# Transposes of q and x moved from TensorE to VectorE in an attention and SwiGLU kernel

## Chip, core and metric

The kernel runs on one core of a Trainium2 chip. The metric is the device time of one execution in microseconds (us), as the median of several runs. Before the change it is 1030.94 us (three runs, 1030.42 to 1032.77). TensorE's granted clock was 1.000 over the whole profile.

Names of the profile: PE is TensorE (matmuls), PEld its weight loads, DVE is VectorE, ACT is ScalarE, POOL is GpSimd, SP is the engine whose queue issues most transfers. "L712" is line 712 of the kernel before; after the change most lines are two higher.

## What is computed

Linear attention without softmax, with a root-mean-square norm for each head, and then a feed-forward block:

```python
kv  = einsum('bhsd,bhse->bhde', k, v)          # batch 8, 8 heads, 576 positions, 64 wide
out = einsum('bhsd,bhde->bhse', q, kv)
x   = out / sqrt(mean(out*out, -1) + 1e-6) * g_norm
x   = x.transpose(0, 2, 1, 3).reshape(4608, 512)
g   = x @ w_gate                               # 512 x 1536
h   = g / (1 + exp(-g)) * (x @ w_val)
y   = h @ w_out                                # 1536 x 512
```

## The kernel before

The 4608 rows are cut into nine blocks of 512 (`blocks`, n = 0 to 8). A block's rows can straddle two batches, so its q comes from two pieces. For each block there is an attention part (class `Att`) and a feed-forward part (class `Ffn`) with an up stage (gate and value products) and a down stage (product with w_out). The attention part of block n+1 is done inside the down stage of block n, between its matmuls.

**Fewer products.** The big matrix products use a Strassen-like scheme: seven products P1 to P7 of half-sized blocks in place of eight, at the price of sums of the operands. S1, S3, S4 and the changed a21 are sums of the moving operand (`sums` for x, `h_sums`, `turn_s3` and the last line of `after2` for h; the last of these is called S4). T2 is a sum of the weights that is made once, in place, in the value weights `wv` (`t2`): one subtraction and one addition for each of six pairs j. Block 0 makes its up stage plainly (`plain_up`), while weights still come in. Block 1 uses the scheme once (class `Up`), and blocks from `DEEP` = 2 on use it twice, one within the other (class `Inner`). The doubled scheme needs further weight sums, called leaves. They are made by VectorE during block 1 (`leaf_steps`) from the weights, stored to DRAM (`w<-t`, `w<-r`, `w<-xi`, L821) and read back by every later block in pieces through the class `Stream` (`t<-w`, L793). GpSimd makes the remaining weight differences (`prepare`, `turn_t`, L112) in the pool `t_pool` with nine tiles, which stream pieces share: `stream.pump` issues a load when the tile that stood nine places earlier is free. `stream.enable(n + 1)` opens a block's loads.

**Order.** Each engine runs its instructions in the order of its queue. A scheduler orders them at build time from the order of the source and from its own view of readiness; `tc.issue_after(x)` holds back what is in its scope until x in that order. TensorE's order in a down stage comes from the loop in `Ffn.down`: with the step list of an attention part that has an entry for 5, it is P1, P6, P5, P7, P2, P4, P3, otherwise P1, P5, P6, P7, P2, P4, P3. After each P the entry of `nxt.steps()` for it is run.

**Two ways for q and x.** The matmuls want q and x with the head dimension on partitions; they come in and go out with rows on partitions.
- On TensorE: q is loaded by rows (`load_q`, four transfers a block), transposed by matmuls with an identity matrix (`turn_q`, L335) and copied out of PSUM. x is transposed in the same way (`turn_x`, L402) and copied out by ScalarE with the gain (L403). Each takes 16 transposes a block. The steps are `half` at P1, `middle` at P6 and `last` at P2: the two halves of the block are normed one after the other.
- On VectorE: q is loaded by 32 small transfers that already put each 32-wide quarter where it belongs (`load_quarters`, L281), so that one instruction a half (STREAM_TRANSPOSE, L329) turns all 32 x 32 blocks in place. For x, two such instructions turn the blocks (`blocks_x`, L412), 16 transfers move them to their partitions (`place_x`, L426, eight each on the queues of SP and ScalarE), and ScalarE applies the gain (`gain_x`, L431). The steps are `whole` at P1 (both products, the norm of all 512 rows, the block transposes), `place_x` at P5 and `end` (gain and sums) at P2.

`TURNED` = 3 is the first block of the second way; block 1 takes the second way for its q alone. In the first way q of a block is loaded late in the up stage before it; in the second it is loaded a block earlier still: `blocks[n + 2].load_q` runs at the start of the down stage of block n.

**Block 0 and 1.** T2 of all six pairs follows the first scaled half of block 1 (`nxt.halves[0]`). In block 1 the leaves of the last two pairs (`latest`) are made behind P1 and P7 of the down stage, both in one buffer named `xi`.

Of the kernel before, what the change touches and what calls it, by code (L numbers as in the profile page):

```python
# [8 lines left out]
F32 = mybir.dt.float32  # L9
# [5 lines left out]
P = 128  # L15
# [3 lines left out]
def kernel(  # L19
# [41 lines left out]
    nc = tc.nc  # L61
# [22 lines left out]
    ld_pool = pool("ld", 4)  # L84
# [23 lines left out]
    wg, wv = ([consts.tile([P, NS, 2 * P], F32, name=f"{x}{j}") for j in range(NP)] for x in ("wg", "wv"))  # L108
# [84 lines left out]
    class Att:  # L193


        def __init__(self, n):
            self.n = n

            self.cut, half = divmod(n, 2)
            self.split = half * D  # L200
            self.ps, self.z = {}, None
            self.q, self.k, self.v, self.room = [], {}, {}, None
            self.halves = []
            self.quarters = n == 1 or n >= TURNED

        def parts(self, t):

# [58 lines left out]
                    )  # L266
                    views[j] = t.rearrange("p h (t d) -> p h t d", t=KT)

        def load_quarters(self, i):


            ld = ld_pool.tile([P, LD], F32, name="ld")[:, 0 : 2 * BLK]
            to = ld.rearrange("p (j g d) -> p j g d", j=2, d=P // 4)
            cut = 2 * self.n
            spans = [(self.n - 1, S - D * self.n, 0, cut), (self.n, 0, cut, BLK // 32)]
            for j in range(2):
                for r in range(4):
                    h, d = divmod(r, 2)
                    for b, s0, g0, g1 in spans:
                        if g1 > g0:  # L280
                            nc.sync.dma_start(  # L281
                                out=to[32 * r : 32 * (r + 1), j, g0:g1],
                                in_=q[b, 4 * i + 2 * j + h, s0 : s0 + 32 * (g1 - g0), 32 * d : 32 * (d + 1)].rearrange(
                                    "(g p) d -> p g d", p=32
                                ),
                            )
            self.q.append(ld)

        def load_q(self, i):
            if self.quarters:  # L290
# [127 lines left out]
        def place_x(self):  # L418
            src = self.turned.rearrange("p i (x c) -> p (i x) c", c=P)
            self.x = x_pool.tile([P, 7, 2, HB], F32, name="x")  # L420
            dst = self.x[:, 0:4].rearrange("p o k (t c) -> p (o k t) c", c=P)
            rows = [slice(32 * r, 32 * (r + 1)) for r in range(4)]
            for a in range(4):
                for b in range(4):
                    queue = nc.scalar if b % 2 else nc.sync
                    queue.dma_start(out=dst[rows[b], :, rows[a]], in_=src[rows[a], :, rows[b]])  # L426

        def gain_x(self):
            for i in range(2):
# [56 lines left out]
        def steps(self):  # L486
# [14 lines left out]

            if self.n >= TURNED:
                return {1: whole, 5: self.place_x, 2: end}
# [19 lines left out]

    DEEP = 2

    TURNED = 3

    class Quad:

# [41 lines left out]
    class Up(Quad):  # L571
# [51 lines left out]
        def multiply(self, p):  # L623
            super().multiply(p)
            ffn = self.ffn
            if ffn.n != DEEP - 1:
                return

            if p == 5:
                self.leaf_room = ring().rearrange("p f (s c) -> p (f s) c", c=P)  # L630
            if p in (5, 7, 4):
                at = 3 * (5, 7, 4).index(p)
                ffn.making.extend(leaf_steps(self.j, [(self.w[p].unsqueeze(1), (p,))], self.leaf_room[:, at:]))
            if p == 3:
                if ffn.leaf_room is None:
                    ffn.leaf_room = x_pool.tile([P, 3, 7, P], F32, name="xi").rearrange("p a b c -> p (a b) c")
                halves = lambda t: t[self.j].rearrange("p (o i) c -> p o i c", o=2)
                steps = leaf_steps(self.j, [(halves(wg), (1, 2)), (halves(wv), (6, 3))], ffn.leaf_room)
                if self.j < NP - 2:
                    ffn.later.extend(steps)  # L640
                else:
                    ffn.latest.append(steps)

# [195 lines left out]
    class Down(Quad):  # L839
# [23 lines left out]
        def multiply(self, p):  # L863
            super().multiply(p)
            if p in self.t:
                stream.free((self.ffn.n, p))
            if p == 4:
                stream.enable(self.ffn.n + 1)
            stream.pump()

# [20 lines left out]
        def after2(self):  # L891
            add(nc.vector, self.o1[:, :, 0:HD], self.ps["a"], self.s)
            if self.final:
                self.ffn.store(self.o1[:, :, 0:HD], 0, slice(0, HD))

            pairs = self.ffn.h.rearrange("p (j e) t -> p e j t", e=2)
            sub(nc.vector, pairs[:, 1, :, 0:HB], pairs[:, 1, :, 0:HB], pairs[:, 0, :, HB:BLK])

        def after7(self):
            o = ring()  # L900
# [25 lines left out]
    class Ffn:  # L926
# [52 lines left out]
        def down(self, nxt):  # L979

            down = self.down_
            fill = nxt.steps() if nxt else {}
            for p in (1, 6, 5, 7, 2, 4, 3) if 5 in fill else (1, 5, 6, 7, 2, 4, 3):
                if p == 1:
                    down.turn_t(7, self.ended)
                if p == 6:
                    down.turn_t(4, nxt.halves[0] if nxt and nxt.n >= TURNED else None)

                with tc.issue_after(nxt.multiplied.ins) if self.n == 0 and p in (5, 6) else ExitStack():
                    down.multiply(p)  # L990
                self.make(12)
                if p == 5 and self.n == DEEP - 1:
                    for i in range(2):
                        self.loads(i)
                if p in fill:
                    fill[p]()
                if p in (1, 7) and self.latest:

                    with tc.issue_after(nxt.scaled.ins):
                        for step in self.latest.pop(0):  # L1000
                            step()
                if p == 1:

                    with tc.issue_after(nxt.q_turned.ins) if self.n == 0 else ExitStack():
                        down.turn_s3()
# [47 lines left out]
    def t2(place, b22, b11):  # L1053

        sub(nc.vector, place, b22, place)
        add(nc.vector, place, place, b11)

    blocks = [Att(n) for n in range(NB)]
# [7 lines left out]
    for n in range(NB):  # L1066
        ffn = Ffn(n, blocks[n])
        nxt = blocks[n + 1] if n + 1 < NB else None
        if n == 0:

            with tc.issue_after(squared.ins), tc.issue_after(scaled.ins):
                weights(2)
            ffn.plain_up(0, (0,))
            copied = blocks[0].copied
            blocks[0].turn_x(1)
            for f in range(NF):
                with tc.issue_after(blocks[0].copied.ins if f else copied.ins):
# [12 lines left out]
            ffn.plain_end()  # L1090
            for g in range(2):
                nxt.kv(g)
        else:

            def third():
                nxt.kv(0)
                nxt.load_kv(1)

            def two_thirds():
                nxt.kv(1)  # L1100
                if nxt.n < TURNED:
                    for i in range(2):
                        nxt.load_q(i)

            ffn.up({4: third, 8: two_thirds} if nxt else {})
        if nxt:
            nxt.turn()
        if 0 < n < NB - 2:
            blocks[n + 2].load_kv(0)
        if TURNED - 2 <= n < NB - 2:  # L1110
            ffn.loads = blocks[n + 2].load_q
            if n >= DEEP:
                for i in range(2):
                    ffn.loads(i)
        ffn.down(nxt)
        if n == 0:
            blocks[2].load_kv(0)

            with tc.issue_after(nxt.halves[0].ins):
                for j in range(NP):  # L1120
                    t2(wv[j][:, 0:2], wv[j][:, 2:4], wg[j][:, 0:2])


# [29 lines left out]
```

## Time and profile before

| Part of the run | start to end, us | length, us |
|---|---|---|
| loads, block 0's attention, weights and up | 0 to 117.79 | 117.79 |
| down of block 0, attention of block 1 inside | 117.79 to 159.85 | 42.06 |
| up of block 1, leaves made | 159.85 to 238.62 | 78.77 |
| down of block 1, attention of block 2 inside | 238.62 to 279.66 | 41.04 |
| blocks 2 to 8 | 279.66 to 1031.2 | 751.5 |

The borders are starts of TensorE's matmuls: P1 of a down stage (b<-wo,h) and the first product of an up stage. The profile's section on busy time has one entry for each engine: microseconds, share of the span, number of instructions. The chain that ended last is followed back from the last instruction, so it tells whose work the end waited for. In the list of waits each line gives the engine and line that waited, what it waited for, the total, the number of times and the longest.

In up of block 1 VectorE is busy 70.3 of 78.8 us and GpSimd 32.0, in down of block 0 37.5 and 19.5 of 42.1, in down of block 1 30.7 and 10.2 of 41.0. SP's queue issued 21 small loads of q in 11.69 us at 109.65, and eight placements of x in 5.76 us at 693.77. The median time from issue to landing was 2.0 us for most of the small q loads, 3.2 us for a placement, 3.6 us for a stream load of 256 KB.

### The profile page before, as it was taken

How to read it: one execution, taken by the hardware profiler on the slowest of the kernel's cores; microseconds unless marked ns; L12 is line 12 of the kernel's file. 1: busy time of each engine (PE TensorE's matmuls, PEld its weight loads, DVE VectorE, ACT ScalarE, POOL GpSimd, SP SyncE). 2: the span in 40 equal slices, each digit the busy share in tenths (PEclk: the TensorE clock that was granted, in tenths of full speed). 3: DMA queues.
4: the chain of work that ended last, by engine and by line, in shares of the span. 5: the costliest groups of instructions: out<-in, count | busy, mean ns of one | idle time of the engine just before them, and what ended most of it. 6: DMA issues, size and time to landing. Idle time of an engine off the chain costs nothing.

```text
span 1031.2 us, 21440 instructions
## 1 busy us (share of the span) xinstructions
PE 1013.0 (98%) x8570; PEld 903.5 (88%) x8570; DVE 703.9 (68%) x1185; ACT 230.2 (22%) x359; POOL 371.6 (36%) x280
## 2 busy tenths in 40 slices
PE   5999999999999999999999999999999999999998
PEld 4544688888899989998999899988999899989997
DVE  2999796997766855585657576674669466856661
ACT  2666111222211211221112122111212111211110
POOL 0000543444035612462156305630455136513670
PEclk9999999999999999999999999999999999999999
DMA  7689614783778456855686468736862666066611
GB/s 215 195 261 266 119 37 128 186 223 72 205 202 248 90 133 209 248 126 114 192 242 163 68 205 240 198 53 186 236 199 50 169 196 193 22 165 205 189 30 41
DMA packets 252403, 168.15 MB, mean 163 GB/s; under 512 B 129168, under 2 KB 220432, under 8 KB 252304
## 3 DMA queue, kind: packets, MB, share of 16 engines
q1 hardware_dynamic: 225808, 163.37, 57.9%
q10 hardware_dynamic: 26432, 3.41, 2.0%
q8 instruction: 68, 1.11, 0.5%
q14 instruction: 31, 0.25, 0.1%
q0 software_dynamic: 64, 0.00, 0.0%
HBM read 138.02 MB, written 22.41 MB: 156 GB/s over the span
## 4 chain that ended last, share of the span: by engine, by line
PE 83%; DVE 10%; DMA 4%; SPq 1%; ACT 1%; issue 1%; DVEq 0%; ACTq 0%
PE b L712 26%; PE b L549 20%; PE c L712 13%; PE c L549 10%; PE a L712 6%; PE a L549 5%; DVE r L153 2%; PE m L355 1%; PE m L314 1%; SPq L281 1%; DVE r L147 1%; DMA h<-in_v_dram 1%; DVE r L152 1%; DMA ld<-in_v_dram 1%; DVE xi L112 1%
## 5 line engine op out<-in xcount | busy, mean ns | idle before, releaser
L111 POOL TENSOR_TENSOR r<-r 128x256 f32<-128x256 f32 (+1 forms) x105 | 110.7, 1060 | 310.1 <-DVE r L111 204.4
L111 DVE TENSOR_TENSOR r<-b,r 128x512 f32<-128x512 f32 (+1 forms) x273 | 162.1, 606 | 64.2 <-PE b L712 59.1
L112 POOL TENSOR_TENSOR t<-wo 128x512 f32<-128x512 f32 x81 | 117.1, 1470 | 191.6 <-DVE wo L111 106.9
L111 DVE TENSOR_TENSOR r<-c,r 128x512 f32<-128x512 f32 (+1 forms) x179 | 108.5, 618 | 95.0 <-PE c L712 55.5
L712 PE MATMUL b<-x,t 128*128 128x128 f32 x1092 | 151.0, 275 | 0.0
L712 PEld LDWEIGHTS b<-x,t 128*128 128x128 f32 x1092 | 136.5, 192 | 0.6
L111 DVE TENSOR_TENSOR r<-a,r 128x512 f32<-128x512 f32 (+1 forms) x99 | 62.5, 631 | 108.7 <-PE a L549 63.0
L712 PE MATMUL c<-xi,t 128*128 128x128 f32 x840 | 112.2, 275 | 0.4 <-DVE xi L111 0.4
L113 POOL TENSOR_TENSOR h<-r 128x1024 f32<-128x1024 f32 (+1 forms) x40 | 82.1, 2067 | 80.6 <-DVE r L111 72.8
L712 PEld LDWEIGHTS c<-xi,t 128*128 128x128 f32 x840 | 102.8, 192 | 0.5 <-DVE xi L111 0.5
L549 PE MATMUL b<-wo,h 128*128 128x256 f32 x432 | 99.5, 382 | 0.1
L549 PE MATMUL b<-t,h 128*128 128x256 f32 x432 | 96.9, 381 | 0.0
L549 PEld LDWEIGHTS b<-t,h 128*128 128x128 f32 x432 | 81.3, 190 | 11.3 <-issue 0.2
L549 PEld LDWEIGHTS b<-wo,h 128*128 128x128 f32 x432 | 79.9, 190 | 12.8 <-DVE h L113 2.5
L726 ACT COPY r<-b 128x512 f32<-128x512 f32 x63 | 36.9, 585 | 211.7 <-PE b L712 199.8
L712 PE MATMUL b<-xi,t 128*128 128x128 f32 x588 | 79.7, 276 | 0.0
L712 PEld LDWEIGHTS b<-xi,t 128*128 128x128 f32 x588 | 72.4, 192 | 0.0
L712 PE MATMUL b<-x,wg 128*128 128x128 f32 x336 | 52.7, 279 | 0.2 <-DVE x L112 0.2
L712 PE MATMUL b<-x,wv 128*128 128x128 f32 x336 | 51.3, 275 | 0.0
L549 PE MATMUL c<-t,s 128*128 128x256 f32 x216 | 48.3, 380 | 0.0
L549 PE MATMUL a<-wo,h 128*128 128x256 f32 x216 | 48.3, 379 | 0.0
L549 PE MATMUL c<-wo,h 128*128 128x256 f32 x216 | 48.1, 379 | 0.0
(131 smaller groups left out, 1579.8 us busy)
## 6 DMA issues: line engine op xcount, KB each, us to landing
t<-w SPq DMA_DIRECT2D x336, 256.0 KB, 3.6
out_dram<-r SPq DMA_DIRECT2D x17, 512.0 KB, 3.1
ld<-in_k_dram SPq DMA_DIRECT2D x26, 288.0 KB, 5.1
ld<-in_v_dram SPq DMA_DIRECT2D x26, 288.0 KB, 5.7
ld<-in_moe_w_gate_dram SPq DMA_DIRECT2D x12, 512.0 KB, 4.6
ld<-in_moe_w_val_dram SPq DMA_DIRECT2D x12, 512.0 KB, 4.4
ld<-in_moe_w_out_dram SPq DMA_DIRECT2D x12, 512.0 KB, 5.3
w<-t SPq DMA_DIRECT2D x18, 256.0 KB, 2.5
```

Of the source, the lines that this page charges most:

```text
L111: add = lambda e, o, a, b: e.tensor_tensor(out=o, in0=a, in1=b, op=OP.add)
L112: sub = lambda e, o, a, b: e.tensor_tensor(out=o, in0=a, in1=b, op=OP.subtract)
L113: mul = lambda e, o, a, b: e.tensor_tensor(out=o, in0=a, in1=b, op=OP.mult)
L147: nc.vector.tensor_scalar(out=mag.bitcast(F32), in0=mag.bitcast(F32), scalar1=self.LOW, scalar2=self.HIGH, op0=OP.max, op1=OP.min,)
L152: nc.vector.tensor_scalar(out=sign, in0=high, scalar1=0x80000000, scalar2=None, op0=OP.bitwise_and)
L153: return nc.vector.scalar_tensor_tensor(out=mag, in0=mag, scalar=3, in1=sign, op0=OP.logical_shift_left, op1=OP.bitwise_xor)
L281: nc.sync.dma_start(out=to[32 * r : 32 * (r + 1), j, g0:g1], in_=q[b, 4 * i + 2 * j + h, s0 : s0 + 32 * (g1 - g0), 32 * d : 32 * (d + 1)]. ...
L314: nc.tensor.matmul(self.kv_ps[r][u * D : (u + 1) * D, g, :], lhsT=k[:, u, c, :], rhs=v[:, u, c, :], start=(c == 0), stop=(c == KT - 1),)
L355: self.multiplied = nc.tensor.matmul(self.ps[i][u][p : p + D, t, j, :], lhsT=self.qt[rows, 2 * i + t, j, p : p + D], rhs=kvs[b % 3][rows, ...
L549: nc.tensor.matmul(banks[e][:, e], lhsT=lhsT, rhs=rhs, start=first and i == 0 and (e == 0 or banks[0] is not banks[1]), stop=i == self.ste ...
L712: nc.tensor.matmul(ps[:, i, f], lhsT=self.weight(o, p, f), rhs=self.operand(o, p), start=first and (i, f) == (0, 0), stop=True, skip_group ...
L726: nc.scalar.copy(out=dst, in_=ps)
```

## The change

Blocks 1 and 2 take the second way, for q and for x: `TURNED` becomes 1 and `quarters` holds for every block but block 0. What goes with it:
- Block 3's q isn't loaded in down of block 1 but in up of block 2, in four parts (`load_quarters` gets the pairs to load).
- Block 2's q is still loaded in up of block 1, now by quarters.
- The leaves of the last two pairs of block 1 are made behind P5 and P7, after the placement of x is issued; the second takes a ring buffer in place of `xi`.
- Half of T2 (pairs 3 to 5) is put behind S4 of block 0's down stage, to leave VectorE to x before.
- A block's stream loads may begin behind P7, not behind P4.
- With `TURNED` = 1 the condition in `turn_t(4, ...)` also holds in block 0: the difference waits for the scaled x of block 1.

It is meant to take transposes off TensorE and to keep what replaces them off its way.

```diff
-            self.quarters = n == 1 or n >= TURNED
+            self.quarters = n > 0
...
-        def load_quarters(self, i):
+        def load_quarters(self, i, pairs=(0, 1)):
-            ld = ld_pool.tile([P, LD], F32, name="ld")[:, 0 : 2 * BLK]
-            to = ld.rearrange("p (j g d) -> p j g d", j=2, d=P // 4)
+            if pairs[0] == 0:
+                self.q.append(ld_pool.tile([P, LD], F32, name="ld")[:, 0 : 2 * BLK])
+            to = self.q[i].rearrange("p (j g d) -> p j g d", j=2, d=P // 4)
...
-            for j in range(2):
+            for j in pairs:
...
-    TURNED = 3
+    TURNED = 1
...
-                steps = leaf_steps(self.j, [(halves(wg), (1, 2)), (halves(wv), (6, 3))], ffn.leaf_room)
+                steps = lambda room: leaf_steps(self.j, [(halves(wg), (1, 2)), (halves(wv), (6, 3))], room)
...
-            if p == 4:
+            if p == 7:
                 stream.enable(self.ffn.n + 1)
...
-                if p == 5 and self.n == DEEP - 1:
-                    for i in range(2):
-                        self.loads(i)
                 if p in fill:
                     fill[p]()
-                if p in (1, 7) and self.latest:
-                    with tc.issue_after(nxt.scaled.ins):
-                        for step in self.latest.pop(0):
+                if p in (5, 7) and self.n == DEEP - 1:
+                    with tc.issue_after(nxt.scaled.ins), tc.issue_after(nxt.placed.ins):
+                        room = self.leaf_room if p == 5 else ring().rearrange("p f (s c) -> p (f s) c", c=P)
+                        for step in self.latest.pop(0)(room):
                             step()
...
-                if nxt.n < TURNED:
+                if nxt.n == 2:
                     for i in range(2):
                         nxt.load_q(i)
-            ffn.up({4: third, 8: two_thirds} if nxt else {})
+            fill = {4: third, 8: two_thirds} if nxt else {}
+            if n == DEEP:
+                for a, at in enumerate((1, 2, 3, 5)):
+                    fill[at] = lambda i=a // 2, j=a % 2: nxt.load_quarters(i, (j,))
+            ffn.up(fill)
...
             with tc.issue_after(nxt.halves[0].ins):
-                for j in range(NP):
+                for j in range(NP // 2):
+                    t2(wv[j][:, 0:2], wv[j][:, 2:4], wg[j][:, 0:2])
+            with tc.issue_after(ffn.down_.s4.ins):
+                for j in range(NP // 2, NP):
                     t2(wv[j][:, 0:2], wv[j][:, 2:4], wg[j][:, 0:2])
```

More of the change, by code (lines that the diff above doesn't have):

```diff
@@ L286, in load_quarters @@
                             )
-            self.q.append(ld)
         def load_q(self, i):
@@ L425, in place_x @@
                     queue = nc.scalar if b % 2 else nc.sync
-                    queue.dma_start(out=dst[rows[b], :, rows[a]], in_=src[rows[a], :, rows[b]])
+                    placed = queue.dma_start(out=dst[rows[b], :, rows[a]], in_=src[rows[a], :, rows[b]])
+                    if b % 2 == 0:
+                        self.placed = placed
         def gain_x(self):
@@ L637, in multiply @@
                 halves = lambda t: t[self.j].rearrange("p (o i) c -> p o i c", o=2)
-                steps = leaf_steps(self.j, [(halves(wg), (1, 2)), (halves(wv), (6, 3))], ffn.leaf_room)
+                steps = lambda room: leaf_steps(self.j, [(halves(wg), (1, 2)), (halves(wv), (6, 3))], room)
                 if self.j < NP - 2:
-                    ffn.later.extend(steps)
+                    ffn.later.extend(steps(ffn.leaf_room))
                 else:
@@ L896, in after2 @@
             pairs = self.ffn.h.rearrange("p (j e) t -> p e j t", e=2)
-            sub(nc.vector, pairs[:, 1, :, 0:HB], pairs[:, 1, :, 0:HB], pairs[:, 0, :, HB:BLK])
+            self.s4 = sub(nc.vector, pairs[:, 1, :, 0:HB], pairs[:, 1, :, 0:HB], pairs[:, 0, :, HB:BLK])
         def after7(self):
@@ L1109 @@
             blocks[n + 2].load_kv(0)
[L1110 to L1114, printed above, removed]
+        if DEEP <= n < NB - 2:
+            for i in range(2):
+                blocks[n + 2].load_q(i)
         ffn.down(nxt)
```

## The prediction

> **What bounds the kernel now.** I read the page's busy shares first, then the chain that ended last, then what TensorE waited for, then the timelines around the places that the change touches.
>
> ```profile
> PE 1013.0 (98%) x8570; PEld 903.5 (88%) x8570; DVE 703.9 (68%) x1185; ACT 230.2 (22%) x359; POOL 371.6 (36%) x280
> PE 83%; DVE 10%; DMA 4%; SPq 1%; ACT 1%; issue 1%; DVEq 0%; ACTq 0%
> ```
>
> TensorE is busy for 98% and owns 83% of the chain. TensorE's waits say how much is left besides its own work:
>
> ```profile
> PE m L248 <- DMA h<-in_v_dram: 5.8, 2, 4.9
> PE b L335 <- DMA ld<-in_q_dram: 4.2, 1, 4.2
> PE a L712 <- DMA t<-w: 0.8, 1, 0.8
> PE c L549 <- DVE r L111: 0.7, 1, 0.7
> ```
>
> 10.0 us lie in the start (first loads), which the diff leaves alone. All later waits are below 1 us each. So a matmul taken off TensorE shortens the run by its issue time, as long as nothing new stops it. The transposes to be removed, in TensorE's timeline (start, length, count, operation):
>
> ```profile
> 135.65 1.04 PE L402 MATMUL m<-ident,r 128*128 128x128 f32 x8
> ...
> 148.62 1.04 PE L402 MATMUL m<-ident,r 128*128 128x128 f32 x8
> ...
> 233.07 0.60 PE L335 MATMUL m<-ident,ld 128*128 128x128 f32 x4
> ...
> 237.75 0.60 PE L335 MATMUL m<-ident,ld 128*128 128x128 f32 x4
> ...
> 255.46 1.04 PE L402 MATMUL m<-ident,r 128*128 128x128 f32 x8
> ...
> 268.42 1.04 PE L402 MATMUL m<-ident,r 128*128 128x128 f32 x8
> ```
>
> Lengths overlap [...]; what counts is the distance between starts.
>
> [...] starts follow at 0.216 us (128x256) and 0.112 us (128x128) almost everywhere. [...] each L412 pair is followed by 16 transfers (L426). [...] two T2 subtractions took 1.28 us at 130.88, two took 3.44 us at 133.28, while GpSimd ran L112 (132.94 to 137.85).
>
> **The parts.**
>
> *1. x of blocks 1 and 2 and q of block 2 leave TensorE.* I compare the down stages by starts. Block 0: P1 starts at 117.79, the next up at 159.85: 42.06 us. A stage of the new kind is read from block 2 (P1 to up at 387.97): both products together 2.02 us (353.84 to 355.86), the product P after them 5.28, each other P 5.18. New block 0: P1 5.38 + the wait for the second L329 (0.46 idle, 0.67 by starts), which stays because the loads of block 1's q are the same + 2.02 + 5.28 + 5 x 5.18 = 39.25. Saved 2.81. Block 1: 238.62 to 279.66 is 41.04; new 5.28 + 2.02 + 5.28 + 25.90 = 38.48. Saved 2.56. The 16 transposes of q in up of block 1 took 0.44 + 0.49 + 0.22 + 0.44 + 0.44 = 2.03 by starts. **Sum 7.40 us**, all on the chain.
>
> *2. What replaces them beside TensorE.* VectorE: 2 q transposes of 1.23 us for one copy of 0.69 (L339), and per block two x transposes (2.36 the pair). The way of x in block 2, which I take as the pattern:
>
> ```profile
> 364.69 2.36 DVE L412 STREAM_TRANSPOSE r<-r 128x1024 f32<-128x1024 f32 x2
> ...
> 367.13 6.73 ACTq L426 DMA_DIRECT2D x<-r  x8
> ...
> 377.32 2.19 ACT L431 ACTIVATE x<-x,gain 128x1024 f32<-128x1024 f32 x2 [2.84 <-DMA x<-r]
> ...
> 379.76 0.68 DVE L111 TENSOR_TENSOR x<-x 128x512 f32<-128x512 f32 x1
> ```
>
> From the end of the products (355.86) to placed and scaled x (379.51) 23.65 us; the up stage follows 32.1 us after the products. In block 0 the products end at 123.17 + 0.67 + 2.02 = 125.86, so x is scaled at 149.5, and VectorE comes out of S4 and the add behind it at 149.7; up starts at 159.85 - 2.81 = 157.0. S1 of x is first read by P5, one P of 1.73 later (158.7).
>
> *3. Half of T2 behind S4.* Six T2 (12 instructions) took 11.5 us of VectorE, 130.88 to 142.41. Now three stand before S4, three after it (P2 ends at about 146.6, S4 at 149). Queued between these three (3 x (0.73 + 1.04) = 5.3 us bare, up to 8.7 at the contended 3.44 + 2.36 for two) are the four sums of x (2.8 us bare, 5.8 contended: 151.11 to 156.82 in the trace). In the built order S1 stands behind three of the six T2 instructions: 149.7 + 2.5 + 0.7 = 152.9 bare, 149.7 + 4.6 + 1.7 = 156.0 contended, against 158.7. Hidden both ways, with 2.7 us left at the worst; a21 (P6, 160.5) has less. I keep 0.3 us for it, less than a quarter of one GpSimd subtraction (1.34).
>
> *4. q of block 2 in quarters.* 32 loads for 4, on SP. In block 0, 21 of these took 11.69 us, 0.56 each, so 32 need 18 us. They stand among the 48 stores of leaves (L821), which wait on VectorE in order; the last 16 stand together in the built queue and hold the stores behind them by 16 x 0.52 (20 took 10.36 at 238.73) = 8.3 us, less the 1.8 us by which the next store follows anyway (213.38, 215.15): 6.5. Behind a store wait a GpSimd difference that reuses its tile (L112 waited 26.5 us for these in five waits) and a leaf buffer. SP catches up by about 222; the q transposes run near 227, the down stage reads near 237. I cost it at nothing, hidden behind up of block 1; the upper bound is 6.5 us less the 3.1 us that GpSimd already waits for such a store at 221.59: 3.4.
>
> *5. Block 3's q in up of block 2, not in down of block 1.* SP work of 32 x 0.56 in a stretch where SP waits for TensorE to free stream tiles. Nothing. It clears SP for the 8 placements there; in block 5 the same loads ended at 693.77 and put placements off to then.
>
> *6. Last leaves behind P5 and P7, the last in a ring buffer.* 16 VectorE instructions after the x transposes, 6.6 us (a set took 3.30, 253.62 to 256.92). In the pattern VectorE is idle 9.84 us there (367.05 to 376.89); the last four (2.0 us) come after S4 and push the sums of x back by as much. The first xi sum would end at 382.53 + 1.02 + 2.0 = 385.6 on the pattern's clock, where P5 reads it at 388.86. Nothing.
>
> *7. Stream loads begun behind P7.* In the order of the queues this changes one place: down of block 5, where the first loads stood behind an output store.
>
> ```profile
> 706.88 0.41 SPq L936 DMA_DIRECT2D out_dram<-r  x1
> 707.40 4.96 SPq L793 DMA_DIRECT2D t<-w  x9
> ...
> 713.82 0.71 PE L712 MATMUL a<-x,t 128*128 128x128 f32 x4 [0.79 <-DMA t<-w]
> ...
> 717.67 2.05 PE L712 MATMUL c<-xi,t 128*128 128x128 f32 x16 [0.39 <-DVE xi L111]
> ```
>
> Now six loads follow the placements directly (699.5). The wait of 0.8 us goes. The next two (0.39 and 0.20) stay: the scaling L431 still stands behind the copy L907 in ScalarE's queue and ran at 706.75. **0.8 us.**
>
> Sum: 7.4 + 0.8 - 0.3 = 7.9; 1030.94 - 7.9 = **1023.0**.
>
> **Rivals.** *A crowded SP in block 1*: the stores come late, GpSimd's differences and VectorE's adds slip, P5 of a unit waits. For it: TensorE already waits 0.74 there for VectorE (213.98), and VectorE is busy 70.3 of 78.8 us. Against: the delay falls late and is made up. 1030.94 - 8.2 + 3.4 = 1026.1. *x late*: placements spread out by traffic, or sums held by contention, in blocks 1 and 2; P5 stands second in the up stage and nothing can go ahead of it. For it: VectorE's queue is in order and the sums of block 1 now share it with T2. Against: 2.7 us left. Four us in each: 1022.7 + 8 = 1030.7, no change. *Slower*: both of these, and 6 us in each block: 1022.7 + 12 = 1034.7. It takes a placement of about 9 us more than the 23.65 measured. *Better*: the waits of block 1 (0.9 + 0.2 by starts) and the two at 717 go too: 1021.0.
>
> **How the numbers follow.** Forecast 0.58, better 0.08, crowded SP 0.22, x late 0.08, slower 0.04. The range takes in the first three: 1021.0 to 1027.0, leaving out 0.12. Faster 0.88, within 0.2% (1028.9 to 1033.0) 0.08, slower 0.04.
>
> **What would show it.** No L402 after the start and no L335 after 40 us; the down stages of blocks 0 and 1 near 39.3 and 38.5 us; no wait of TensorE for t<-w near 706; VectorE some 7 us busier. Wrong would be: waits of TensorE above 1 us at the first P5 of blocks 1 or 2, waits for VectorE in up of block 1 above the 1.1 us of now, or L329 waiting for q in block 1.

## The result, and the profile after

The changed kernel takes **1025.23 us** (median of four runs, 1025.01 to 1026.59) against 1031.03 (1030.42 to 1032.77) for the kernel before on the same chip: ratio 0.9944, 95% interval 0.9927 to 0.9961. It is 5.8 us faster where 7.9 were forecast. A repeat, told below, gave 0.9946 (0.9934 to 0.9959).

The profiled executions differ by more, 1031.2 and 1023.2. Of this difference of about 7.9 us, 1.45 lie ahead of P1 of block 0, in the wait for the first loads, which put P1 at 117.79 us before, at 116.34 after and at 117.44 in the repeat, and has nothing to do with the change. So I compare from P1 of block 0 to the last instruction: 913.14 before, **906.68** after (907.14 in the repeat), **6.0 to 6.5 us saved**.

The page's busy shares and its chain by engine, after:

```profile
PE 1006.5 (98%) x8522; PEld 896.9 (88%) x8522; DVE 701.0 (69%) x1168; ACT 228.0 (22%) x352; POOL 368.9 (36%) x280
PE 92%; DVE 3%; DMA 2%; SPq 1%; issue 1%; ACT 1%; DVEq 0%; ACTq 0%
```

TensorE has 48 matmuls fewer (16 for q, 32 for x) and owns 92% of the chain where it had 83%. Its waits after (engine, what was waited for, us, times, longest):

```profile
PE m L248 <- DMA h<-in_v_dram: 4.7, 2, 3.9
...
PE c L551 <- DVE r L111: 1.6, 3, 0.7
```

The wait for t<-w is gone. The wait for VectorE's running sum, 0.7 in one place before, is 1.6 in three: that is the first sign of where gain was lost. Stage by stage, from matmul start to matmul start ("spread" is the experiment x5, "spread twice" x11; a row named for a block has its up and its down stage):

| Stage | before | after | repeat | spread | spread twice |
|---|---|---|---|---|---|
| down of block 0 | 42.06 | 39.51 | 39.78 | 39.50 | 39.50 |
| up of block 1 and P1 of its down stage | 84.05 | 82.76 | 82.96 | 81.88 | 81.96 |
| rest of down of block 1 | 35.76 | 34.13 | 34.13 | 34.13 | 34.13 |
| block 2 | 108.31 | 108.49 | 108.49 | 107.83 | 107.83 |
| block 6 | 109.65 | 108.43 | 108.44 | 108.55 | 106.86 |
| P1 of block 0 to the end | 913.14 | 906.68 | 907.14 | 905.24 | 903.63 |

Block 6 runs from the first product of its up stage to that of block 7; it is what the texts below call the stretch from block 5 to 6. Blocks 3 to 5, 7 and 8 agree to 0.05 us in every kernel, so a single profile shows a stage's change well, while the whole time does not. Two stages are exceptions. Up of block 1 moves by 0.6 us between profiles of like kernels (84.05 and 83.44 before; 82.41 to 82.96 after). Down of block 0 carries a wait of TensorE for block 1's second q transpose (L329), whose loads land at varying times: by starts it cost 0.67 us before, nothing after, 0.29 in the repeat and 0.93 in x2.

**The account.** TensorE's time from each start to the next, summed by line from down of block 0 to the end of block 2, before and after: attention products of blocks 1 and 2 (L355) 6.19 and 4.06; transposes of x (L402) 3.68 and 0; of q (L335) 2.02 and 0. That is 7.83 us taken off. The kv products (L314) rise from 5.56 to 6.29, the P products from 250.82 to 252.62 (1.2 of these 1.8 us in up of block 1, 0.4 in block 2): 2.53 us come back. 5.30 remain, and with 1.22 at block 6 the sum is 6.5. The attention products fall because each block's stood in two groups before, one of them with the 0.67 us wait for L329 in it, and now stand in one of 2.03. That this wait is gone is luck, and 0.67 of the 6.5 us with it. The kv products stood in five groups and now stand in eight; by estimate every group costs some 0.24 us beyond its matmuls, from the times of three groups after (72 at 202.38 took 1.21, 34 at 144.66 took 0.72, 14 at 317.37 took 0.38).

**The way of x in block 1**, beside TensorE, in the timelines of VectorE, ScalarE and TensorE after (start, length, engine, operation):

```profile
131.28 2.36 DVE L412 STREAM_TRANSPOSE r<-r 128x1024 f32<-128x1024 f32 x2
...
133.72 7.41 ACTq L426 DMA_DIRECT2D x<-r  x8
...
143.38 2.19 ACT L433 ACTIVATE x<-x,gain 128x1024 f32<-128x1024 f32 x2 [1.62 <-DMA x<-r]
...
157.58 1.89 PE L551 MATMUL c<-x,t 128*128 128x256 f32 x8
```

The first P5, at 157.58, has no bracket, so it waits for nothing. x is scaled at 145.57, 21.8 us after the products end (123.75), and its last sum ends at 156.3.

**The lost part**, at the end of up of block 1 after, one line each from the timelines of SP, SP, VectorE and TensorE:

```profile
209.60 9.55 SPq L282 DMA_DIRECT2D ld<-in_q_dram  x16
219.25 0.42 SPq L823 DMA_DIRECT2D w<-r  x1
...
222.90 1.03 DVE L112 TENSOR_TENSOR xi<-wv 128x512 f32<-128x512 f32 x2 [0.92 <-DMA w<-xi]
...
232.31 1.99 PE L551 MATMUL c<-x,wv 128*128 128x256 f32 x8 [0.55 <-DVE r L111]
```

Sixteen q loads hold SP for 9.55 us. The leaf stores (L823) behind them go out late; VectorE waits 0.92 us to write a new leaf into a buffer that such a store still reads; and everything in VectorE's queue slips, the running sum included that P3 of the last unit needs. Four profiles have this run of 16 loads at over 9 us, and in them VectorE's wait for the store and TensorE's stall at the last unit (by starts) go together: 0.92 and 0.71, 0.68 and 0.48 in the repeat, 0.59 and 0.37 in x6, 0.61 and 0.39 in x9.

### The profile page after: what moved, and what is told of

The parts are those of the page before. It is cut to its first block, busy times and chain, and to the rows that moved or that the text cites. A ratio compares the mean times of both kernels' runs of the same rounds, so it can differ in the third digit from the quotient of the medians.

```text
span 1023.2 us, 21404 instructions
## 1 busy us (share of the span) xinstructions
PE 1006.5 (98%) x8522; PEld 896.9 (88%) x8522; DVE 701.0 (69%) x1168; ACT 228.0 (22%) x352; POOL 368.9 (36%) x280
## 4 chain that ended last, share of the span: by engine, by line
PE 92%; DVE 3%; DMA 2%; SPq 1%; issue 1%; ACT 1%; DVEq 0%; ACTq 0%
PE b L714 26%; PE b L551 20%; PE c L714 13%; PE c L551 10%; PE a L714 6%; PE a L551 5%; PE b L1018 4%; PE c L1018 4%; PE m L314 2%; PE m L355 1%; DMA h<-in_v_dram 1%; SPq L282 1%; DVE xi L112 1%; DVE r L111 1%; DMA h<-in_k_dram 0%
## 5 line engine op out<-in xcount | busy, mean ns | idle before, releaser
L112 POOL TENSOR_TENSOR t<-wo 128x512 f32<-128x512 f32 x81 | 114.5, 1437 | 213.4 <-DVE wo L111 103.5
```

## Experiments

All are edits of the changed kernel unless said otherwise. "From P1" is the time from P1 of block 0 to the end in the profile; 906.7 to 907.1 for the changed kernel.

**The changed kernel again (x0_after_again).** No edit.

> The changed kernel once more, for a narrower interval and to see which stage lengths repeat. Its trace gave 8.0 us less than that of before, of which 1.45 lay in the start (first loads), while the timed medians differ by 5.8. If the start is chance, the ratio is near 0.9940 to 0.9945 and the stages repeat: down of block 0 39.5 us, up of block 1 with P1 82.8, rest of down of block 1 34.1. If the start belongs to the change, P1 of block 0 again comes about 1.4 us earlier than before.

1025.56 us (1024.57 to 1027.35), ratio 0.9946 (0.9934 to 0.9959). The stalls near 195 and 209 us and at the last unit of up of block 1 were 0.76, 0.89 and 0.48 us by starts, in the first profile 0.50, 0.90 and 0.71. The loss comes each time, its parts vary. P1 of block 0 came at 117.44, near the 117.79 of before, so the earlier start in the first profile was chance.

**Block 2's q back on TensorE (x1_q2_on_tensor).**

```diff
-            self.quarters = n > 0
+            self.quarters = n > 0 and n != 2
```

> Block 2's q by rows and transposed on TensorE as before the change, its x still on VectorE. Measured by up of block 1 with P1 of its down stage (84.05 before, 82.76 changed, 81.54 if only what was taken away counted; 1.22 lost). Theory (the 1.22 is the price of q by quarters and on VectorE): the 16 transposes cost 2.03 again and the 1.22 comes back, 83.6. Rival (the loss comes from the rest of the change, such as the other order of P1 or the split of kv): 84.8.

1026.78 us (1026.40 to 1027.17), ratio 0.9957 (0.9941 to 0.9972). Up of block 1 with P1 is 83.44, with one stall near 211 (0.89); block 2 is 107.83; from P1 906.67. That is the theory's 83.6, not the rival's 84.8. So taking q of block 2 off TensorE, 2.02 us of matmuls, earned nothing as it was built: the 0.5 to 0.7 that it gained in up of block 1 was lost in block 2, which here is 0.66 shorter, with its kv products in one group fewer.

**Block 2's q by four large loads (x2_q2_few_loads).** Loads by rows, transposes still on VectorE: block 2 then computes with q in the wrong places, and only the times are of use.

```diff
         def load_quarters(self, i, pairs=(0, 1)):
...
+            if self.n == 2:
+                for t in range(2):
+                    tile_ = self.q[i][:, BLK * t : BLK * (t + 1)].rearrange("p (h d) -> p h d", h=H)
+                    for b, s0, p0, p1 in self.parts(2 * i + t):
+                        nc.sync.dma_start(out=tile_[p0:p1], in_=q[b, :, s0 : s0 + p1 - p0, :].rearrange("h p d -> p h d"))
+                return
```

> Block 2's q in 4 large loads by rows in place of 32 small ones, still transposed by VectorE, so block 2's rows of the output are those of a misplaced q (that part of the computation is changed). It takes the crowd off SP and leaves VectorE's two transposes. Theory SP (stores of leaves come late behind 16 loads in a row, VectorE waits 0.92 us for one and is late with an add): up of block 1 with P1 81.6 to 81.9, no wait of VectorE for w<-xi, in all about 1.0 us less than the changed kernel. Theory VectorE (2.45 us more work in a full stage): 82.6 to 82.8, the wait of 0.71 us before P3 of the last unit stays.

1024.72 us (1023.45 to 1026.13), ratio 0.9937 (0.9923 to 0.9950); up of block 1 with P1 82.42, block 2 107.83, from P1 906.57. The stall at the last unit is gone, as the SP theory wants, but the stage is between the two expectations: the stalls near 196 and 210 (0.84 and 0.88) stayed. Down of block 0 was 40.44, since the products waited for L329, 0.93 us by starts. Inconclusive on the size.

**Half of the loads on ScalarE's queue (x3_two_queues).**

```diff
-                            nc.sync.dma_start(
+                            (nc.scalar if self.n == 2 and d else nc.sync).dma_start(
```

> Half of block 2's 32 loads of q issued from ScalarE's queue, so that SP has 16. Theory SP: the longest run of loads on SP halves, up of block 1 with P1 about 82.0, if 16 issues of 0.5 to 0.8 us on ScalarE don't hold its copies out of PSUM. Theory VectorE: 82.7. If ScalarE's copies are held: over 83, with waits of TensorE for copies by ScalarE.

1026.05 us (1024.80 to 1027.75), ratio 0.9950 (0.9937 to 0.9964); up of block 1 with P1 82.95, from P1 907.36 (1.04 of it in down of block 0, at the wait for L329). ScalarE's timeline and TensorE's:

```profile
188.33 2.66 ACTq L282 DMA_DIRECT2D ld<-in_q_dram  x4
191.03 0.59 ACT L571 COPY r<-b 128x512 f32<-128x512 f32 x1 [4.11 <-DMA ld<-in_q_dram]
...
191.76 1.97 PE L551 MATMUL b<-x,t 128*128 128x256 f32 x8 [2.23 <-ACT r L571]
```

The stalls for VectorE are gone, all three, but a copy out of PSUM stands behind four loads in ScalarE's queue, and TensorE waits 2.23 us for it. This wait comes ahead of the three places and gives VectorE time there, so the run doesn't tell what the shorter run of loads on SP is worth. Here four loads on the queue of an engine that also computes took 2.66 us ahead of that copy.

**Only block 1's x, on the kernel before (x4_block1_x_alone).**

```diff
-            if self.z is None or 0 < self.n < TURNED:
+            if self.z is None or self.n == 2:
...
-            if self.n >= TURNED:
+            if self.n == 1 or self.n >= TURNED:
```

(and the same condition where `turn_t(4, ...)` is called, and T2 split as in the change.)

> The kernel before with one part: x of block 1 goes to VectorE and the placing transfers, and half of T2 stands behind S4 for it. Block 2's q and x stay on TensorE, block 3's q and the stream loads as before. Theory (the gain of x is that of the transposes taken off TensorE, and nothing comes back): down of block 0 falls from 42.06 us to 39.2 to 39.9 (2.81 us of transposes away, 17 kv matmuls of 0.36 us moved in from the up stage, the 0.67 us wait for the second q transpose may or may not be there); up of block 1 with the down stage behind it stays at 119.81 less these 0.36, up of block 1 up to the products (84.05 before) at 83.4 to 84.0; blocks 2 to 8 as before (108.3, 107.8, ..., 109.65). Time about 1028.5. Rival (the stalls that up of block 1 shows in the changed kernel come from x and T2 sharing VectorE): up of block 1 up to the products 84.6 or more, with stalls of TensorE near 195 and 232 us, and time 1029.5 or more.

1029.18 us (1027.99 to 1029.88), ratio 0.9976 (0.9967 to 0.9985). Down of block 0 is 39.51: the step alone gives its 2.55 us. Up of block 1 with P1 is 84.17, a little above the 83.4 to 84.0 of the theory and below the rival's 84.6; a stall of 0.84 near 197 stands where the profile before had 0.23. An unlooked-for number: block 6, which this edit leaves alone, is 109.17 and not 109.65, because the wait for t<-w is 0.32 and not 0.79:

```profile
710.75 0.71 PE L712 MATMUL a<-x,t 128*128 128x128 f32 x4 [0.32 <-DMA t<-w]
```

So that wait itself varies by half a microsecond.

**Block 2's q loads spread over up of block 1 (x5_q2_spread).**

```diff
             def two_thirds():
                 nxt.kv(1)
-                if nxt.n == 2:
-                    for i in range(2):
-                        nxt.load_q(i)
...
+            if n == 1:
+                def q2(more, i, j):
+                    more()
+                    nxt.load_quarters(i, (j,))
+
+                for a, at in enumerate((2, 4, 6, 8)):
+                    fill[at] = lambda more=fill.get(at, lambda: None), i=a // 2, j=a % 2: q2(more, i, j)
```

> The changed kernel, but block 2's 32 q loads are asked for in four groups of 8 from P-unit 1 of the up stage on, instead of all at two thirds of it: in the order of SP's queue 8 stand before and 8 behind the 8 placements of block 1's x, and no run of 16 is left among the leaf stores. The second kv load comes behind two leaf stores. The kv products in up of block 2 stand in two groups again. Theory (the run of 16 loads holds the leaf stores, these GpSimd, that VectorE, that TensorE): the 0.71 us stall at the last unit of up of block 1 is gone and up of block 1 up to the products falls from 82.8 to 81.6 to 82.2; block 2 is 107.83 instead of 108.49; time about 1024.2. Rival (the stalls of up of block 1 come from VectorE and GpSimd [...], whatever SP does): up of block 1 up to the products stays at 82.4 to 83.0, only block 2 gains, time about 1024.9. Second rival (loads ahead of the placements, 8 x 0.56 = 4.5 us, make block 1's x late): TensorE waits 1 us or more at the first P5 of block 1, up of block 1 at 83.5 or more, time at 1026 or more.

1024.47 us (1023.83 to 1025.40), ratio 0.9934 (0.9918 to 0.9951). Up of block 1 with P1 is 81.88, inside the SP theory's 81.6 to 82.2 and below the rival's 82.4; block 2 is 107.83; from P1 905.24. The last stretch of SP's queue, to set against the 16 loads above:

```profile
208.95 0.38 SPq L823 DMA_DIRECT2D w<-t  x1
209.37 2.04 SPq L282 DMA_DIRECT2D ld<-in_q_dram  x4
211.51 0.42 SPq L823 DMA_DIRECT2D w<-r  x1
```

The r store that went at 219.25 goes at 211.51, VectorE no longer waits for an xi store, and the stall at the last unit is gone. The eight loads that now stand behind the placements of block 1's x (141.34, 3.91 us) cost nothing. The two kernels that keep this edit gave 81.91 and 81.96: the number repeats, against a mean of 82.64 for the profiles of the stage as changed (82.76, 82.96, and 82.41 and 82.43 from the next kernel and x9). So the edit is worth **0.7 us**, but not all of it is the crowded SP. The stall at the last unit, 0.37 to 0.71 and **0.5** on average, is what the run of 16 loads cost. Stalls of 0.50 and 0.43 stay near 195 and 209. The second of these was 0.9 in all four profiles of the stage as changed and also in the profile before, and the running sum that it waits for stands ahead of the run of 16. It shrank as one leaf sum came to stand behind this running sum, and not ahead of it (VectorE in the changed kernel, then here):

```profile
208.49 0.42 DVE L112 TENSOR_TENSOR xi<-wg 128x256 f32<-128x256 f32 x1
...
209.03 0.69 DVE L111 TENSOR_TENSOR r<-c,r 128x512 f32<-128x512 f32 x1
```

```profile
208.81 0.68 DVE L111 TENSOR_TENSOR r<-c,r 128x512 f32<-128x512 f32 x1
...
210.61 0.41 DVE L112 TENSOR_TENSOR xi<-wg 128x256 f32<-128x256 f32 x1
```

The three spread kernels have this order (0.43, 0.56 and 0.56 us), all others the first. A new delay near 222 us takes some 0.2 us back.

**Stream loads begun behind P4 again (x6_stream_at_p4).** `if p == 7:` becomes `if p == 4:`.

> The changed kernel with the stream's loads begun behind P4 again, as before. Theory (the 1.22 us that the stretch from block 5 to 6 lost comes from this part alone): that stretch is 109.65 us again instead of 108.43, with a wait of TensorE for t<-w of 0.8 to 1.0 us and two small ones behind it; all else as in the changed kernel (block 2 at 108.5, blocks 3 to 5 at 107.8, blocks 7 and 8 at 104.5 and 105.5). Rival (part of it came with the other parts, above all by the place of block 3's q loads or the order of the leaves): the stretch is 109.2 or less.

1027.22 us (one run). Block 6 is 109.27, between the two expectations. The wait for t<-w is back with 0.63 us by starts. All else is as in the changed kernel.

**T2 whole, ahead of S4 (x7_t2_whole).**

```diff
-                for j in range(NP // 2):
+                for j in range(NP):
                     t2(wv[j][:, 0:2], wv[j][:, 2:4], wg[j][:, 0:2])
-            with tc.issue_after(ffn.down_.s4.ins):
-                for j in range(NP // 2, NP):
-                    t2(wv[j][:, 0:2], wv[j][:, 2:4], wg[j][:, 0:2])
```

> The changed kernel with T2 of the value weights whole behind the first half of the products, as before, so that all 12 of its instructions stand before S4 on VectorE. Theory (the split is hidden either way): down of block 0 is 39.5 to 40.5, up of block 1 up to the products 82.3 to 83.3, no wait of TensorE over 1 us near 150 to 160. Rival (S4 and with it the sums of x come late without the split): a wait of TensorE of 1 us or more at the first P5 of up of block 1 or at the end of down of block 0, and down of block 0 and up of block 1 together 1.5 us or more longer than in the changed kernel (39.51 + 82.76). Second rival (the split itself costs, by T2 beside the sums): the two together 1 us or more shorter.

1028.32 us (one run). Down of block 0 is 43.72, 4.21 us longer; with up of block 1 behind it 3.39 longer. VectorE's timeline and TensorE's:

```profile
147.28 2.35 DVE L111 TENSOR_TENSOR wv<-wv,wg 128x512 f32<-128x512 f32 x2
149.55 0.68 DVE L111 TENSOR_TENSOR r<-a,r 128x512 f32<-128x512 f32 x1
150.15 2.22 DVE L112 TENSOR_TENSOR h<-h 128x1536 f32<-128x1536 f32 x1
152.30 0.68 DVE L111 TENSOR_TENSOR r<-c,r 128x512 f32<-128x512 f32 x1
...
153.03 7.13 PE L551 MATMUL c<-wo,h 128*128 128x256 f32 x24 [2.26 <-DVE r L111]
```

The twelve T2 instructions ran until 149.6, so S4 (L112 of h) began at 150.15 and not at 145.38, and the sum behind it freed its bank 2.26 us too late for P3. My first theory here, hidden either way, fell: without the split, 3.4 of the 6 us would be lost. Up of block 1 with P1 is 81.94 here, below the 82.41 to 82.96 of the changed kernel. Its 16 loads on SP took 7.94 us:

```profile
213.59 7.94 SPq L282 DMA_DIRECT2D ld<-in_q_dram  x16
```

VectorE doesn't wait for an xi store behind them, and the stall at the last unit is gone without any spreading. So the run of loads cost TensorE time where VectorE met the late store (0.37 to 0.71 us in the four profiles above) and none here, where it met none; why it met none, by the shorter run or by the time that TensorE's wait gave, isn't shown.

**Block 7's q loads behind the placements (x8_q2_spread_q7_late).** On top of x5:

```diff
-        if DEEP <= n < NB - 2:
+        if DEEP <= n < NB - 2 and n != 5:
...
         ffn.down(nxt)
+        if n == 5:
+            with tc.issue_after(nxt.placed.ins):
+                for i in range(2):
+                    blocks[n + 2].load_q(i)
```

> Block 2's q loads spread as before (x5_q2_spread), and block 7's 32 q loads, which in the changed kernel stand ahead of the placements of block 6's x on SP, are asked for behind them. In ScalarE's queue the scaling of block 6's x then stands ahead of the copy that follows P7 of the down stage, and the last kv products of block 7 come later. Theory (the waits of 0.60 and 0.36 us that are left at the start of block 6 come from x scaled behind that copy): both waits go, the stretch from block 5 to 6 falls from 108.4 to 108.5 to 107.4 to 107.7, the rest as in x5_q2_spread (up of block 1 up to the products 81.9, block 2 107.83); time about 1023.5. Rival (the loads now stand among the stream's loads, and hold some t<-w, or q of block 7 comes late for its transposes): a new wait of TensorE for t<-w of 0.5 us or more in block 6, the stretch from 5 to 6 and block 6 together no shorter, time 1024.5 or more.

1029.59 us (1027.98 to 1030.70), ratio 0.9981 (0.9973 to 0.9989): the rival was right, and larger than it said. The waits for xi and x at the start of block 6 are gone, but block 6 is 113.14 (SP's timeline, then TensorE's):

```profile
704.15 14.63 SPq L282 DMA_DIRECT2D ld<-in_q_dram  x27
718.88 10.08 SPq L795 DMA_DIRECT2D t<-w  x14
...
721.80 2.08 PE L714 MATMUL b<-x,t 128*128 128x128 f32 x8 [3.86 <-DMA t<-w]
```

27 small loads in a row hold the stream for 14.63 us. It is the trouble of block 1 again, in another place.

**Block 3's q loads in down of block 1, as before (x9_q3_in_down1).** The four entries of `fill` for block 3 go, and `ffn.loads` is called in down of block 1 behind P5, as in the kernel before.

> The changed kernel with block 3's q loads asked for in down of block 1, as before, most of them ahead of the placements of block 2's x in SP's queue. Theory (20 such loads take 10 us and are through about when x is transposed; the later place of these loads is worth nothing by itself): placements of block 2's x at most 3 us later, no wait of TensorE of 1 us or more at the first P5 of block 2, block 2 at 107.8 to 108.5 (its kv products stand in other groups), time within 0.7 us of the changed kernel's. Rival (clearing SP was needed for x): x scaled 8 to 10 us later, a wait of 1 us or more at the first P5 of block 2, and down of block 1 with block 2 1 us or more longer.

1025.47 us (one run). SP's timeline and TensorE's:

```profile
236.72 21.57 SPq L282 DMA_DIRECT2D ld<-in_q_dram  x32
258.40 6.31 SPq L426 DMA_DIRECT2D x<-r  x8
...
275.32 0.68 PE L714 MATMUL b<-x,wv 128*128 128x128 f32 x4 [0.50 <-DVE x L112]
```

The placements of block 2's x begin at 258.40 and not at 250.75; the scaling then falls behind a copy in ScalarE's queue and comes 6.0 us later. Two stalls of 0.66 and 0.35 us by starts open block 2, and from the start of block 2's attention products to the end of block 2 it is 0.84 us more, though the kv products stand in one group fewer. Against x5, which has as many groups as this kernel, it is 1.5 more. Between the two expectations: the move was needed, for 0.8 us as built and about 1.5 with like groups.

**Only the stream's start, on the kernel before (x10_before_stream_p7).** `if p == 4:` becomes `if p == 7:`.

> The kernel before with one part: the stream's loads are begun behind P7. Theory (this part alone takes the wait for t<-w at the start of block 6 away): the stretch from block 5 to 6 is 108.4 instead of 109.65 (109.17 in x4_block1_x_alone, which differs from the kernel before by nothing there, so 0.7 to 1.2 us), and all other stages are as before. Rival (the place of block 3's q or the leaves had a share in it): 108.9 or more.

1031.43 us (one run); block 6 is 108.43, as expected, and block 2 onward is otherwise as before. With the 109.17 to 109.65 without it, this part is worth **0.7 to 1.2 us**, and it is the whole of what block 6 gained.

**Block 7's q loads spread as well (x11_q7_in_up6).** On top of x5, they get four places in up of block 6 in the way that block 3's have in up of block 2:

```diff
-            if n == DEEP:
-                for a, at in enumerate((1, 2, 3, 5)):
+            if n in (DEEP, 6):
+                for a, at in enumerate((1, 2, 3, 5) if n == DEEP else (3, 5, 6, 7)):
...
-        if DEEP <= n < NB - 2:
+        if DEEP <= n < NB - 2 and n != 5:
```

> As x8_q2_spread_q7_late, but block 7's q loads are asked for in four groups of 8 through up of block 6: in the order of SP's queue 8 stand ahead of the placements of block 6's x, the others in groups of at most 8 among the stream's loads of up of block 6; no run of 27 stands ahead of t<-w. Theory (the 4.07 us wait for t<-w of x8 came from that run of 27 loads at 0.54 us each, and the two small waits from x scaled behind the copy after P7): both are gone, the stretch from block 5 to 6 is 107.4 to 107.8, block 6 behind it 104.5; with the spread loads of block 2 the time is about 1023.5. Rival (any such loads among the stream's hold a t<-w long enough): a wait for t<-w of 0.5 us or more remains in block 6, and time is 1024.5 or more.

**1022.46 us** (1021.78 to 1023.64), ratio 0.9917 (0.9903 to 0.9930). From P1 it is 903.63, shorter than x5 and the changed kernel; the intervals of its ratio and x5's overlap. ScalarE's timeline:

```profile
692.56 2.19 ACT L433 ACTIVATE x<-x,gain 128x1024 f32<-128x1024 f32 x2 [2.36 <-DMA t<-w]
698.48 0.59 ACT L909 COPY r<-b 128x512 f32<-128x512 f32 x1 [3.74 <-PE b L551]
```

Block 6's x is scaled ahead of the copy that waits for P7, no wait is left at the start of block 6, and block 6 is 106.86, shorter than the 107.4 to 107.8 expected: 0.96 us for the two waits, and 0.6 more that I can only put beside the one other difference there, kv products in groups of 38 and 72 in place of 16, 22 and 72. Against the changed kernel, 0.80 in up of block 1, 0.66 in block 2 and 1.57 here make 3.03 of the 3.05 us by which it is shorter from P1.

## Why the prediction was right, and where not

Direction and range held; the size was 7.9 for 5.8. The measured time lies nearer to the rival with the crowded SP (1026.1) than to the forecast's 1023.0, and that rival's mechanism was at work, at a smaller size. Stage by stage, gain in the first profile and forecast:

- down of block 0: 2.55 for 2.81. Some 0.9 went to kv products that moved in; 0.67 came by luck, since the wait for L329, which the step kept, didn't show.
- up of block 1 with P1: 1.29 for 2.03. The kv products that left gave 0.48; new stalls took 1.2.
- rest of down of block 1: 1.63 for 2.56. Again 0.93 for kv products.
- block 2: 0.18 lost where nothing was forecast. Block 6: 1.22 for 0.8.

*Step 1, x and q off TensorE (7.40): right in mechanism, too large in its sum.* The transposes and cut-up products were worth 7.83 us, 0.67 of it the lucky wait. What the step left out are the kv products: 34 each moved into the down stages of blocks 0 and 1, and in eight groups the same number of them took 0.73 us more than in five. The stage that served as its pattern has such a group: from its products (353.84) to the next up stage (387.97) it took 34.13 us, just what the rest of down of block 1 takes after, while the step's sum for this stretch is 33.20. With block 2's kv products in groups of 38 and 72 (x5) in place of 38, 58 and 14, that stage is 0.66 shorter. The built order shows such fillers, and the step put no price on them.

*Step 2, the way of x hidden: right.* 21.8 us from products to scaled x against 23.65, and no wait at P5 (x4 shows the same alone).

*Step 3, half of T2 behind S4, 0.3 us: right that it is hidden; the 0.3 doesn't show.* The pair of T2 subtractions that took 3.44 us in the profile before did so while GpSimd ran L112; that GpSimd made it so long was the step's estimate, not shown. VectorE is through with T2 and the sums of x at 156.90 and then waits 1.64 us for TensorE. x7 adds what the step didn't see: whole, T2 would have cost 3.4.

*Step 4, q of block 2 in quarters, nothing: wrong.* This is the step whose mechanism failed. It had SP catch up by about 222; SP issued without a pause until 236. The cost is some 0.5 us (the stall at the last unit, gone in x5), inside the bound of 3.4. The chain through SP, VectorE's leaf buffer and the running sum is the one the rival named, save that GpSimd's wait, 26.5 us in the prediction and 32.7 after, is still 30.4 in x5 and so is not what mattered. What stays open: of the 2.5 us taken off up of block 1 (2.02 of q and 0.48 of kv) the changed kernel kept 1.1 (mean 83.75 and 82.64) and the spread one 1.8. Part of the other 0.7 lies in the stall of P3 near 195 us, where VectorE is late: it is 0.35 to 0.50 in the spread kernels, 0.35 to 0.76 in the changed one, 0.23 and none in two profiles of that stage as before. The leaf sums run long at times (in x5 two sums of 128x256 took 1.48 and 1.38 us at 204.39, where others took 0.42), and why they do so in one profile and not in the next stays open.

*Step 5, block 3's q later, nothing: right for the forecast.* x9 puts a number on what it prevents, 0.8 to 1.5 us.

*Step 6, last leaves, nothing: right.* Block 2's x sums begin at 266.41, right behind the last leaves, and P5 of block 2 shows no wait.

*Step 7, stream, 0.8: right.* 0.7 to 1.2 by x6 and x10. The two waits that the step said would stay did stay (0.39 and 0.19), and for the reason given: x11 put the scaling ahead of the copy, and they went.

*VectorE some 7 us busier: wrong,* it is 2.9 less. The transposes cost what was said (L412 14.2 to 18.9, L329 17.2 to 19.6). But x on VectorE is normed once a block and not in halves: L373 to L385 fell from 31.3 to 25.1. And the subtractions of x fell from 19.5 to 16.5; why isn't shown.

## What to carry to other kernels

When a slow bulk transfer becomes many small ones, price the queue it is issued from, not the transfer: a run of 16 small loads held up what stood behind it on SP for 9.55 us in the changed kernel, a run of 27 for 14.63 us in x8, and spreading the same loads in groups of eight or fewer cost nothing that these runs show. Such a run cost TensorE nothing where it waited for nothing behind it: the changed kernel keeps 15 such loads at 236.65 (11.50 us), and TensorE shows no wait from 238.61 to 275. Ask of every queue what else lives in it: on SP the loads held stores and with them buffers, on ScalarE they held a copy that TensorE waited for. And where each stage repeats to 0.05 us, judge a part by its stage, not by the whole time.

## What the runs showed of the hardware

A short stall cost more than its length in x7. TensorE waited 2.26 us, 2.43 by starts; the 24 matmuls behind the wait then took 7.13 us, where the 24 ahead of it (145.32) took 5.45. Together that is 4.1 of the 4.21 us by which the stage grew. The granted clock was below 1.00 behind this wait, and in x8 at the end of the wait of 3.86 us for t<-w and behind it, but not in x3 at the wait of 2.23 us. Neighbouring stretches of x7, x8 and x3 (from and to, length, busy time and instructions of TensorE with its matmuls, of its weight loads, of VectorE, ScalarE and GpSimd, then granted clock, share of DMA, GB/s):

```profile
148.00:153.00 5.00, 2.77 (x13) 2.09 (x11) 5.00 (x5) 0.59 (x1) 4.74 (x3) 1.00 0.00 0
153.00:157.00 4.00, 3.97 (x11) 3.17 (x12) 3.04 (x4) 0.00 (x0) 0.50 (x1) 0.57 0.35 131
157.00:160.00 3.00, 3.00 (x15) 2.64 (x14) 0.00 (x0) 0.00 (x0) 0.00 (x0) 1.00 0.00 0
...
717.00:721.50 4.50, 0.94 (x14) 0.68 (x14) 0.42 (x1) 0.00 (x0) 0.08 (x1) 0.99 0.57 133
721.50:724.00 2.50, 2.20 (x10) 2.20 (x11) 0.02 (x1) 0.00 (x0) 0.00 (x0) 0.50 0.94 305
724.00:728.00 4.00, 4.00 (x33) 3.75 (x33) 2.81 (x5) 1.06 (x1) 0.73 (x1) 0.90 1.01 333
...
189.00:191.70 2.70, 0.54 (x3) 0.14 (x1) 2.70 (x4) 0.59 (x1) 2.11 (x2) 1.00 1.14 309
191.70:195.00 3.30, 3.23 (x15) 2.90 (x16) 3.27 (x4) 0.59 (x1) 2.24 (x2) 1.00 0.70 114
```

In x7 the clock was 0.57 on average from 153 to 157 us and 1.00 from 157 to 160. In x8 it was 0.50 from 721.5 to 724 and 0.90 on average in the four us after. From these lines I estimate the loss against a clock of 1.00 at 1.7 us in x7 (0.43 of 4.00 us) and as much in x8 (0.01 of 4.50, 0.50 of 2.50 and 0.10 of 4.00 us). The waits of x7 and x3 are alike in length, 2.26 and 2.23 us, and in x3 the clock stayed at 1.00; what sets the two apart isn't shown.
